# A chunked attention feeding a four-expert layer: the second pair's attention computed two tiles at a time

## The chip, the cores and the metric

The kernel runs on one core of one Trainium2 chip. The metric is the device time of one execution in microseconds (us). A tile is 128 tokens. TensorE is called PE in the profile (its weight loads PEld), VectorE DVE, ScalarE ACT, GpSimd POOL, and SyncE, whose queue issues all DMAs here, SP.

## The reference

Attention within chunks of 64 positions, then a mixture of four experts whose weights multiply every token:

```
scores = q_c @ k_c^T / 8            # 8 batches x 8 heads x 9 chunks, 64 x 64 each
attn   = exp(scores - rowmax); attn = attn / (rowsum + 1e-9)
x      = (attn @ v_c), heads side by side        # 4608 tokens x 512
p      = domain_probs / (rowsum + 1e-9)
out    = sum over e of p[:, e] * (relu(x @ w1[e]) @ w2[e])   # w1 512x1024, w2 1024x512
```

All inputs and outputs are float32.

## The kernel before

**Blocks and passes.** The 36 tiles are taken as one block of 512 tokens and then four pairs of blocks, 1024 tokens (8 tiles) to a pair. The code numbers the pairs 0 to 3; "the second pair" is pair 1. For every block or pair the kernel makes eight passes, n, one for each half of an expert's 1024 hidden columns: passes 0 to 7 belong to the first block, 8 to 15 to pair 0, 16 to 23 to pair 1, and so on to 39. While the passes of one pair run, the attention of the next pair is put between their products: pair 1's attention lies in passes 9 to 14, pair 2's in passes 17 to 21, pair 3's in 25 to 29.

**A pass.** Every float32 factor is split into a high and a low part (ACT rounds off `hi`, POOL or DVE subtracts to get `lo`), and a product is three matmuls for each 128 rows. In the pairs, blocks of 2 by 2 are multiplied with seven products instead of eight, which needs sums and differences of the blocks (`s1` to `s4` of the weights, `t1` to `t4` of the other side). A step is one such product: six matmuls of 128x512. A pass has 28 steps, in an order written out by hand; `g` and `h` are the two halves of x @ w1, `a` and `b` those of the second product for the pass before:

```
WOVEN = ("a1 g1 a2 g2 g6 a5 g5 a6 a3 g7 a7 g4 g3 a4 h1 h2 "
         "b1 b5 h6 b6 b3 h5 b7 h7 b2 b4 h4 h3").split()
```

Counted from 0, step 13 is `a4`, step 17 `b5`, step 20 `b3`, step 21 `h5`, step 22 `b7`, step 25 `b4`. `later_pass` keeps a table `at`: what hangs on step i is issued to the engines right after that step, in the order in which it was added to the table. Each engine works through its own queue in order. `a1, a6, a7, a4`, and likewise `b1, b6, b7, b4`, add up in one PSUM bank, A1; after each of them DVE adds the bank to an accumulator in SBUF (`Outer.add`, L983), and the next of the four may not write the bank before that read.

**w1's factors in pair 0.** In passes 9 to 14 the split factors of w1 are made on the chip. `half_load(n + 1, g)` loads a half of w1's raw blocks into `scratch`, a buffer of 4096 columns: 512 columns of its own (`scratch[0][:, :SUB]`) and then 14 pieces of 256 columns, seven for each half g. `half_sum` (L573, DVE) computes s1 to s4 into pieces; `make` (L590 on ACT, L591 on POOL) splits two pieces at a time, the seven units k = 0 to 6 at steps 20, 26 of a pass and 2, 8, 11, 14, 17 of the next, and `keep_made` stores them for the later pairs. Before, the loads of half 0 hang on step 5 and its sums on steps 11 or 15, 21, 21, 21; half 1's sums are DVE's at steps 9, 9, 10, 11 of the pass that uses them.

**Attention in pair 0's passes (pair 1's tiles).** One tile at a time (`attend`, `a_next`): a burst on PE holds the 16 64x64 products of one tile's `attn @ v` and the 16 of the next tile's scores, between two steps of the pass. It hangs on step 11 or 23, following TILES: nine bursts in all, the first with scores alone, the last with values alone. Between bursts: maximum and difference on DVE (L308, L313), exp on ACT (L319), sums and scaling and a 32x32 transpose on DVE (L322 to L329, L188), and `a_place`, five ACT copies from PSUM to SBUF (L194, L198). ACT copies the result to `scratch[0][:, :SUB]` (L221, L222), and SP stores it from there to `x_kept` in DRAM; pass 15 loads all of it back (`x_back`).

**Attention in the later passes (pairs 2 and 3).** `attend_two` takes two tiles to a burst, always behind step 12: values of tiles t-2 and t-1, scores of t and t+1; five bursts in all. Both tiles' scores lie in `psa`, two PSUM banks, the first tile in columns 0 to 255 of both, the second in 256 to 511. The first tile's softmax hangs on step 13, its scaling and transpose (`two_weights`) on 17, its `a_place` and then the second tile's softmax on 21, the second tile's weights and place on 6 and 9 of the next pass.

Of the kernel before, what the change touches and what calls it, by code (L numbers as in the profile page):

```python
# [15 lines left out]
P = 128  # L16
# [15 lines left out]
def chunk_attention_moe(ctx: ExitStack, tc: tile.TileContext, qk, v, v0, dp, w1, w2, out):  # L32
# [89 lines left out]

    def a_load_v(t, odd=(False, True)):
        s = st[t]
        if not odd[0]:
            s["v"] = load.tile([P, 2 * HG, C], F32, name="v_in")
        to, of = (
            a.rearrange("p (g i h) d -> p g i (h d)", g=2, i=2) for a in (s["v"], v[t - NT])
        )
        if not odd[0]:  # L130
            nc.sync.dma_start(out=to[:, :, 0], in_=of[:, :, 0])
        if odd[-1]:
            for half in range(2):
                rows, other = slice(half * C, (half + 1) * C), slice((1 - half) * C, (2 - half) * C)
                nc.sync.dma_start(out=to[rows, :, 1], in_=of[other, :, 1])

    def a_load_after(t):
        if (t + 1 - NT) % (PAIR * NT):
            a_load(t + 1)

    def quarters():
# [7 lines left out]
    def of_half(i):  # L149
        return slice(i * C, (i + 1) * C)  # L150
# [4 lines left out]

    def a_scores(t):
        s = st[t]
        s["sc"] = blocks(0)
        for c, half, slot, head in quarters():
            q, k = (s["x"][of_half(c), head // HG, x, head % HG] for x in range(2))  # L160
            nc.tensor.matmul(s["sc"][of_half(half), c, slot], lhsT=q, rhs=k, start=True, stop=True)  # L161

    def a_less_max(t):
# [8 lines left out]

    def a_sums(t):
        z = psa[:, 0, HG * C : HG * C + 2 * HG].rearrange("p (c j) -> p c j", c=2)
        st[t]["r"] = inverse_sums(st[t]["sc"], z)

    def a_scale(t):
# [3 lines left out]
        scale(s["e"], s["sc"], s["r"])  # L181

    def a_weights(t):
        a_sums(t)
        a_scale(t)

# [15 lines left out]

    def a_values(t):

        s = st.pop(t)
        av = blocks(1)
        for c, half, slot, head in quarters():
            nc.tensor.matmul(  # L208
                av[of_half(slot % 2), half, head // 2], lhsT=s["v"][of_half(half), head],
                rhs=s["pt"][of_half(half), c, slot], start=True, stop=True,  # L210
            )

    def a_copy(t):
        pair, i = divmod(t - NT, PAIR * NT)
        if pair == 1:
            tile_x = scratch[0][:, :SUB].rearrange("p (j q) -> p j q", j=NK)
        else:
            tile_x = of_tiles(pair, i, 1)[:, 0]
        to = tile_x.rearrange("p j (c q) -> p c j q", c=2)
        av = blocks(1)  # L220
        nc.scalar.copy(out=to[:, :, 0::2], in_=av[:, :, 0::2])  # L221
        nc.scalar.copy(out=to[:, :, 1::2], in_=av[:, ::-1, 1::2])  # L222
        if pair == 1:
            nc.sync.dma_start(out=x_kept[:, i], in_=tile_x)

# [8 lines left out]

    def two_load(t, i):
        if i == 0:
            a_load(t)
            return
        pair = (t - NT) // (PAIR * NT)
        to = of_tiles(pair, 6, 2).rearrange("p g (x i) (j s) -> p g x (i j) s", x=2, s=C)  # L240
        st[t] = {"x": to}
        nc.sync.dma_start(out=to, in_=qk[t].rearrange("g c d x h s -> (c d) g x h s"))

    def two_load_v(t, i, odd):
        if i and not odd:
            pair, j = divmod(t - NT, PAIR * NT)
            st[t]["v"] = of_tiles(pair, 7 if j == 7 else 5, 1)[:, 0].rearrange("p j (h d) -> p j h d", h=2)
        elif not odd:
            st[t]["v"] = load.tile([P, NK, 2, C], F32, name="v_in")
        to = st[t]["v"].rearrange("p (g i) h d -> p g i h d", i=2)  # L250
        of = v[t - NT].rearrange("p (g i h) d -> p g i h d", g=2, i=2)
        if not odd:
            nc.sync.dma_start(out=to[:, :, 0], in_=of[:, :, 0])
            return
        for half in range(2):
            rows, other = slice(half * C, (half + 1) * C), slice((1 - half) * C, (2 - half) * C)
            nc.sync.dma_start(out=to[rows, :, 1], in_=of[other, :, 1])
# [17 lines left out]
    def two_next(t, scores, banks=("B1", "C1")):  # L275
# [15 lines left out]
        if av:  # L291
            pair, j = divmod(t - NT, PAIR * NT)
            to = of_tiles(pair, j, 2).rearrange("p i j (c q) -> p i j c q", c=2)
            for half in range(2):
                for odd in range(2):
                    nc.scalar.copy(out=to[:, :, odd::2, half ^ odd], in_=av[half][:, :, odd::2])

    x_kept = dram.tile([P, PAIR * NT, NK, P], F32, name="x_kept")
# [32 lines left out]
    def attention(pair):  # L331
# [14 lines left out]
        for t in range(first, last, 2):  # L346
# [16 lines left out]
            two_next(t, t + 2 if t + 2 < last else None, (None, None))  # L363

    def a_next(t, after):

        if t is not None:
            a_values(t)
        if after is not None:
            a_scores(after)  # L370

        if t is not None:
            a_copy(t)

# [218 lines left out]
    def make_before(k):  # L598

        if not before:  # L600
            before.append(load.tile([P, 2, *UNIT[1:]], F32R, name="qk_in"))
        src, hi = staged.pop(0), before[0][:, k] if k < 2 else scratch[0][:, :SUB].bitcast(F32R).rearrange(
            "p (u b c) -> p u b c", u=2, c=P
        )
        nc.scalar.copy(out=hi, in_=src)
# [961 lines left out]
    def probs_load(n, s):  # L1567
# [17 lines left out]

    EARLY, LATE = (6, 9, 11), (17, 21, 24)
    TILES = {
        1: ((LATE, 0),), 2: ((EARLY, 1),), 3: ((EARLY, 2), (LATE, 3)), 4: ((EARLY, 4),),
        5: ((EARLY, 5), (LATE, 6)), 6: ((EARLY, 7),),
    }  # L1590
    ALONE = "a1 b1 a2 a5 b5 a6 b6 a3 b7 b2 a7 b3 a4 b4".split()
# [4 lines left out]

    def loads(at, i, t):

        for after, f in enumerate((
            lambda: a_load_v(t, (False,)), lambda: a_load_v(t, (True,)), lambda: a_load_after(t),  # L1600
        )):
            later.append((i + 2 + after, f)) if i + 2 + after >= len(WOVEN) else add(at, i + 2 + after, f)


    later = []

    def attend(at, pair, places, i):
        t = (1 + pair * PAIR) * NT + i
        after = t + 1 if i + 1 < PAIR * NT else None
        if i == 0:  # L1610
            add(at, 13, lambda: a_next(None, t))
            add(at, 14, lambda: a_softmax(t))
            loads(at, 13, t)
        add(at, places[0], lambda: a_weights(t), lambda: a_transpose(t))
        add(at, places[1], lambda: a_place(t))
        add(at, places[2], lambda: a_next(t, after))
        if after:
            add(at, places[2] + 1, lambda: a_softmax(after))
            loads(at, places[2], after)

    def attend_two(at, pair, r):

        t0 = (1 + pair * PAIR) * NT
        if r == 0:
            add(at, 12, lambda: two_load(t0 + 1, 1))
        if not 1 <= r <= 5:
            return
        t, burst = t0 + 2 * (r - 1), 12
        if r > 1:
# [3 lines left out]
        if r < 5:  # L1633
            add(at, burst + 1, lambda: a_softmax(t))
            add(at, 17, lambda: two_weights(t))
            add(at, 21, lambda: a_place(t), lambda: a_softmax(t + 1))
            for i in range(2):
                for odd in range(2):
                    add(at, burst + 2 + 2 * i + odd, lambda i=i, odd=odd: two_load_v(t + i, i, odd))
                if r < 4:  # L1640
                    add(at, burst + 6 + i, lambda i=i: two_load(t + 2 + i, i))
# [53 lines left out]
    def later_pass(n, ahead, late, held):  # L1695
# [247 lines left out]
```

## Time and profile before

| | |
|---|---|
| median of 3 runs | 1463.19 us (1462.77 to 1464.83) |
| profiled execution | 1462.92 us, its span 1461.1 us, 1.8 us around it |
| DVE, ACT, POOL busy over the span | 1080.0, 623.8, 975.8 us |
| pass 11 (302.5 to 343.4 us): PE, DVE, ACT, POOL busy | 40.88, 35.51, 21.36, 32.97 us |
| pass 18 (579.0 to 619.4 us): PE, DVE, ACT, POOL busy | 40.40, 31.16, 16.98, 22.04 us |
| DMA share of pass 11 and of pass 18 | 0.73 and 0.70 |

A row of the timeline has start and length in us, engine, line, operation, out<-in, count, and in brackets how long the engine stood idle before it and what ended that. A row of the chain has start, length and what ran. An `x6` of L758 is one step. f32 products are recorded as two instructions each, so 16 products are x32.

### The profile page before, as it was taken

The page shows a single profiled execution, that of the slowest core. Times are in us where ns is not written, and L with a number is a line of the kernel's source. Part 1 is how long each engine was busy: PE and PEld are TensorE (multiplying, and loading weights), DVE is VectorE, ACT ScalarE, POOL GpSimd, SP SyncE. Part 2 cuts the span into 40 slices and gives each one's busy share as a digit, 9 for nine tenths or more (in the row PEclk, how much of TensorE's full clock was granted, in tenths as well). Part 3 has the DMA queues.
Part 4 walks back from the last instruction along what each step waited for, and adds up shares of the span by engine and source line. Part 5 has one row for each costly group of instructions (what it writes and reads, how often), then busy time and mean ns, then how long its engine had stood idle before and what let it go on. Part 6 is the DMA issues. An engine that isn't in the chain of part 4 may idle for free.

```text
span 1461.1 us, 23404 instructions
## 1 busy us (share of the span) xinstructions
PE 1454.8 (100%) x8574; PEld 1198.8 (82%) x8574; DVE 1080.0 (74%) x1500; ACT 623.8 (43%) x1169; POOL 975.8 (67%) x728
## 2 busy tenths in 40 slices
PE   9999999999999999999999999999999999999998
PEld 7888888888888888888888888888888888888887
DVE  6566758888887986777767977777668856666666
ACT  5556545544554434444423434444334343223332
POOL 6878888888888775455557665655557655555555
PEclk9999999999999999999999999999999999999999
DMA  9899697868779689666565688675566785565555
GB/s 324 302 341 325 256 343 229 278 233 274 236 250 345 219 256 287 233 221 209 189 205 197 230 222 282 218 243 196 197 201 202 206 249 197 199 201 200 204 189 157
DMA packets 198994, 348.51 MB, mean 239 GB/s; under 512 B 70224, under 2 KB 109408, under 8 KB 198496
## 3 DMA queue, kind: packets, MB, share of 16 engines
q1 hardware_dynamic: 198880, 347.02, 72.1%
q8 instruction: 68, 1.11, 0.3%
q14 instruction: 46, 0.38, 0.1%
HBM read 275.59 MB, written 71.38 MB: 237 GB/s over the span
## 4 chain that ended last, share of the span: by engine, by line
PE 97%; POOL 1%; issue 1%; DVE 0%; DMA 0%; ACT 0%; SPq 0%; POOLq 0%; ACTq 0%
PE A L758 50%; PE C L758 27%; PE B L758 15%; POOL hf L448 1%; PE psa L264 1%; PE B L283 1%; PE psa L208 0%; DMA w<-hf 0%; POOL wf L448 0%; PE psa L161 0%; PE C L1256 0%; PE C L283 0%; PE C L1279 0%; PE A L1256 0%; PE B L1164 0%
## 5 line engine op out<-in xcount | busy, mean ns | idle before, releaser
L936 POOL TENSOR_TENSOR hf<-wraw,hf 128x512 fp32r<-128x512 f32 x384 | 508.1, 1341 | 226.3 <-ACT hf L933 225.1
L758 PE MATMUL A<-hf,wf 128*128 128x512 f32 x1536 | 391.4, 390 | 0.0
L758 PE MATMUL A<-xh,wf 128*128 128x512 f32 (+1 forms) x1120 | 386.9, 389 | 0.0
L933 ACT CAST hf<-wraw 128x512 fp32r<-128x512 f32 x384 | 233.3, 622 | 291.0 <-DVE wraw L927 99.5
L758 PEld LDWEIGHTS A<-hf,wf 128*128 128x128 f32 x1536 | 286.5, 188 | 61.9 <-DVE acc L983 1.9
L758 PEld LDWEIGHTS A<-xh,wf 128*128 128x128 f32 x1120 | 210.0, 188 | 43.9 <-POOL wf L591 0.3
L821 ACT COPY s<-A 128x512 f32<-128x512 f32 x192 | 112.7, 587 | 291.2 <-PE A L758 290.9
L758 PE MATMUL A<-xl,wf 128*128 128x512 f32 (+1 forms) x560 | 217.4, 388 | 0.0
L983 DVE TENSOR_TENSOR acc<-A,acc 128x512 f32<-128x512 f32 x232 | 157.9, 681 | 64.5 <-PE A L758 64.1
L758 PE MATMUL C<-xh,wf 128*128 128x512 f32 (+1 forms) x584 | 201.7, 389 | 0.1
L758 PE MATMUL C<-hf,wf 128*128 128x512 f32 x768 | 194.7, 389 | 0.0
L758 PEld LDWEIGHTS C<-hf,wf 128*128 128x128 f32 x768 | 144.2, 188 | 29.9
L758 PEld LDWEIGHTS C<-xh,wf 128*128 128x128 f32 x584 | 109.4, 188 | 23.2 <-DVE B L956 0.5
L927 POOL TENSOR_TENSOR wf<-wraw,wf 128x512 f32<-128x512 f32 x31 | 40.0, 1292 | 129.2 <-DVE wf L921 128.4
L758 PEld LDWEIGHTS A<-xl,wf 128*128 128x128 f32 x560 | 105.2, 188 | 21.7
L936 POOL TENSOR_TENSOR hf<-wf,hf 128x512 fp32r<-128x512 f32 x64 | 90.7, 1418 | 47.2 <-ACT hf L933 47.2
L758 PE MATMUL B<-xh,wf 128*128 128x512 f32 (+1 forms) x344 | 115.4, 384 | 0.0
L983 DVE TENSOR_TENSOR acc<-C,acc 128x512 f32<-128x512 f32 x120 | 82.7, 689 | 43.2 <-PE C L758 40.3
L758 PE MATMUL C<-xl,wf 128*128 128x512 f32 (+1 forms) x292 | 113.3, 388 | 0.0
L927 DVE TENSOR_TENSOR wraw<-wf,wraw 128x512 f32<-128x512 f32 x64 | 94.7, 1479 | 5.5 <-POOL hf L936 4.3
L758 PE MATMUL B<-hf,wf 128*128 128x512 f32 x384 | 97.8, 390 | 0.0
L927 POOL TENSOR_TENSOR wraw<-wraw 128x512 f32<-128x512 f32 x63 | 91.8, 1458 | 0.0
(255 smaller groups left out, 1982.1 us busy)
## 6 DMA issues: line engine op xcount, KB each, us to landing
wf<-w SPq DMA_DIRECT2D x402, 512.0 KB, 4.2
w<-wf SPq DMA_DIRECT2D x46, 512.0 KB, 5.3
w<-hf SPq DMA_DIRECT2D x28, 512.0 KB, 6.6
w<-hf SPq DMA_DIRECT2D x42, 256.0 KB, 5.3
qk_in<-in_qk SPq DMA_DIRECT2D x20, 512.0 KB, 6.1
wf<-in_w SPq DMA_DIRECT2D x19, 512.0 KB, 6.5
xraw<-in_qk SPq DMA_DIRECT2D x14, 512.0 KB, 7.3
ws<-p_t SPq DMA_DIRECT2D x24, 256.0 KB, 4.1
```

Of the source, the lines that this page charges most:

```text
L264: nc.tensor.matmul(s["sc"][of_half(half), c, slot], lhsT=q, rhs=k, start=True, stop=True)
L283: nc.tensor.matmul(av[half][of_half(slot % 2), i, head // 2], lhsT=s["v"][of_half(half), head // 2, head % 2], rhs=s["pt"][of_half(half), ...
L448: eng.tensor_tensor(out=t[1], in0=src, in1=t[0].bitcast(F32), op=ALU.subtract)
L758: nc.tensor.matmul(out, lhsT=lhs(k, a), rhs=rhs(k, b), start=first and i == 0, stop=last and i == len(parts) - 1, skip_group_check=not (fi ...
L821: nc.scalar.copy(out=t, in_=self.a)
L927: (eng or nc.vector).tensor_tensor(out=self.values[place, k], in0=self.values[a, k], in1=self.values[b, k], op=op)
L933: nc.scalar.copy(out=self.part(name, 0)[:, k], in_=self.values[name, k])
L936: (eng or nc.gpsimd).tensor_tensor(out=self.part(name, 1)[:, k], in0=self.values[name, k], in1=self.part(name, 0)[:, k].bitcast(F32), op=A ...
L983: nc.vector.tensor_tensor(out=acc[key], in0=src, in1=acc[key], op=ALU.add)
```

## The change

Pair 1 takes `attend_two` as well, with five bursts, in passes 10 to 14, behind step 13 instead of 12. The second tile of a burst has no buffer of its own: its q and k go to pieces 0 to 3, loaded in halves at steps 22 and 27 of the pass before (behind the makes at 20 and 26 that read these pieces), its v to pieces 4 and 5 at steps 3 and 4 (behind the make at step 2). The result of the first tile goes to the 512 columns in front, that of the second to pieces 2 and 3 (the last burst: 4 and 5), and one DMA stores both.

Since pieces 0 to 5 are taken until the burst, the loads of half 0 of w1 move from step 5 to step 13, behind the burst, and s1 of half 0 from 11 or 15 to 20. Half 1's sums go from DVE to POOL in passes 10 to 14. In pass 14 three raw loads of w2 go to pieces at steps 3, 4 and 10 instead of `e`, `pt`, `v_in` at 9, 12, 12, and the third made unit goes to `v_in`. Pass 9 keeps its old places for w1. The single-tile functions (`attend`, `a_next`, `a_values`, `a_copy` and others) are gone.

```
+        if pair == 1:
+            if groups.start == 0:
+                to = pieces(0, 4).rearrange("p a b c -> p (a b c)")
+                st[t] = {"x": to.rearrange("p (g x h s) -> p g x h s", g=2, x=2, h=HG)}
+            nc.sync.dma_start(
+                out=st[t]["x"][:, groups],
+                in_=qk[t, groups].rearrange("g c d x h s -> (c d) g x h s"),
+            )
+            return
...
+            if pair == 1:
+                to = pieces(4, 2).rearrange("p a b c -> p (a b) c")
...
+                n = 3 * SUB if j == PAIR * NT - 2 else 2 * SUB
+                two = scratch[0][:, : 2 * n].rearrange("p (i x) -> p i x", i=2)[:, :, :SUB]
...
+            if pair == 1:
+                nc.sync.dma_start(out=x_kept[:, j : j + 2], in_=two)
...
     def attend_two(at, pair, r):
         t0 = (1 + pair * PAIR) * NT
-        if r == 0:
+        if pair == 1:
+            if 0 <= r <= 3:
+                for g, i in enumerate((22, 27)):
+                    add(at, i, lambda g=g: two_load(t0 + 2 * r + 1, 1, slice(g, g + 1)))
+            if 1 < r <= 5:
+                for odd in range(2):
+                    add(at, 3 + odd, lambda odd=odd: two_load_v(t0 + 2 * r - 3, 1, odd))
+        elif r == 0:
             add(at, 12, lambda: two_load(t0 + 1, 1))
         if not 1 <= r <= 5:
             return
-        t, burst = t0 + 2 * (r - 1), 12
+        t, burst = t0 + 2 * (r - 1), 13 if pair == 1 else 12
...
-            for i in range(2):
+            for i in range(1 if pair == 1 else 2):
...
         elif pair == 0:
-            for places, i in TILES.get(n % n_pass, ()):
-                attend(at, pair + 1, (17, 20, 23) if places == LATE else places, i)
+            attend_two(at, pair + 1, n % n_pass - 1)
...
         if n + 1 < 2 * n_pass - 1:
-            add(at, 5, lambda: half_load(n + 1, 0))
+            add(at, 5 if n == n_pass + 1 else 13, lambda: half_load(n + 1, 0))
             add(at, 13, lambda: half_load(n + 1, 1, (0,)))
             add(at, 19, lambda: half_load(n + 1, 1, (1,)))
-            half_sums(at, 0, (11 if n % n_pass in (3, 5) else 15, 21, 21, 21))
+            half_sums(at, 0, (15 if n == n_pass + 1 else 20, 21, 21, 21))
         if n_pass < n < 2 * n_pass - 1:
-            half_sums(first, 1, (5, 6, 9, 10) if n == n_pass + 1 else (9, 9, 10, 11))
             if n == n_pass + 1:
+                half_sums(first, 1, (5, 6, 9, 10))
                 half_sums(first, 0, (None, None, None, 3))
+            else:
+                half_sums(first, 1, (9, 9, 10, 11), nc.gpsimd)
...
-            (2 * n_pass - 2, (), ((9, att, "e"), (12, att, "pt"), (12, load, "v_in"))),
+            (2 * n_pass - 2, (), ((3, None, 0), (4, None, 2), (10, None, 6))),
```

More of the change, by code (lines that the diff above doesn't have):

```diff
@@ L121, in a_load @@
         nc.sync.dma_start(out=s["x"], in_=qk[t].rearrange("g c d x h s -> (c d) g x h s"))
[L123 to L139, printed above, removed]
     def quarters():
@@ L154, in blocks @@
         return psa[:, :, i * HG * C : (i + 1) * HG * C].rearrange("p c (j k) -> p c j k", k=C)
[L156 to L161, printed above, removed]
     def a_less_max(t):
@@ L171, in a_softmax @@
         a_exps(t)
-    def a_sums(t):
-        z = psa[:, 0, HG * C : HG * C + 2 * HG].rearrange("p (c j) -> p c j", c=2)
-        st[t]["r"] = inverse_sums(st[t]["sc"], z)
     def a_scale(t):
@@ L181, in a_scale @@
         scale(s["e"], s["sc"], s["r"])
-    def a_weights(t):
-        a_sums(t)
-        a_scale(t)
     def a_transpose(t):
@@ L201, in a_place @@
                 )
[L203 to L224, printed above, removed]
     def x_tiles(pair):
@@ L233, in of_tiles, with two_load @@
         return (xraw[pair] if pair in xraw else x_tiles(pair))[:, i : i + n]
-    def two_load(t, i):
+    def two_load(t, i, groups=slice(0, 2)):
         if i == 0:
@@ L246, in two_load_v @@
             pair, j = divmod(t - NT, PAIR * NT)
-            st[t]["v"] = of_tiles(pair, 7 if j == 7 else 5, 1)[:, 0].rearrange("p j (h d) -> p j h d", h=2)
+            if pair == 1:
+                to = pieces(4, 2).rearrange("p a b c -> p (a b) c")
+            else:
+                to = of_tiles(pair, 7 if j == 7 else 5, 1)[:, 0]
+            st[t]["v"] = to.rearrange("p j (h d) -> p j h d", h=2)
         elif not odd:
@@ L292, in two_next @@
             pair, j = divmod(t - NT, PAIR * NT)
-            to = of_tiles(pair, j, 2).rearrange("p i j (c q) -> p i j c q", c=2)
+            if pair == 1:
+                n = 3 * SUB if j == PAIR * NT - 2 else 2 * SUB
+                two = scratch[0][:, : 2 * n].rearrange("p (i x) -> p i x", i=2)[:, :, :SUB]
+                two = two.rearrange("p i (j q) -> p i j q", j=NK)
+            else:
+                two = of_tiles(pair, j, 2)
+            to = two.rearrange("p i j (c q) -> p i j c q", c=2)
             for half in range(2):
@@ L363, in attention @@
             two_next(t, t + 2 if t + 2 < last else None, (None, None))
[L365 to L373, printed above, removed]
     KEYS = {"a11": 0, "a12": 1, "a22": 2, "s1": 3, "s2": 4, "s3": 5, "s4": 6}
@@ L598, in make_before @@
     def make_before(k):
[L600 to L604, printed above, removed]
+        if k == 0:
+            t = load.tile([P, 2, *UNIT[1:]], F32R, name="qk_in")
+            before.extend(t[:, i] for i in range(2))
+        elif k == 2:
+            before.append(load.tile(UNIT, F32R, name="v_in"))
+        src, hi = staged.pop(0), before[k]
         nc.scalar.copy(out=hi, in_=src)
@@ L625, in raw_load @@
     def raw_load(pool, name):
-        k, t = unstaged.pop(0), pool.tile([P, 2, 2, P], F32, name=name)
+        k, t = unstaged.pop(0), pool.tile([P, 2, 2, P], F32, name=name) if pool else pieces(name, 2)
         staged.append(t)
@@ L1583, in chunk_attention_moe @@
     )
[L1586 to L1590, printed above, removed]
     ALONE = "a1 b1 a2 a5 b5 a6 b6 a3 b7 b2 a7 b3 a4 b4".split()
@@ L1595, in first_load @@
             a_load((1 + pair * PAIR) * NT)
[L1597 to L1602, printed above, removed]
-    later = []
[L1607 to L1619, printed above, removed]
+    later = []
     def attend_two(at, pair, r):
         t0 = (1 + pair * PAIR) * NT
-        if r == 0:
+        if pair == 1:
+            if 0 <= r <= 3:
[5 more added lines that the diff above has]
+        elif r == 0:
             add(at, 12, lambda: two_load(t0 + 1, 1))
@@ L1737, in later_pass @@
         elif pair == 0:
-            for places, i in TILES.get(n % n_pass, ()):
-                attend(at, pair + 1, (17, 20, 23) if places == LATE else places, i)
+            attend_two(at, pair + 1, n % n_pass - 1)
         late = []
         if n + 1 < 2 * n_pass - 1:
-            add(at, 5, lambda: half_load(n + 1, 0))
+            add(at, 5 if n == n_pass + 1 else 13, lambda: half_load(n + 1, 0))
             add(at, 13, lambda: half_load(n + 1, 1, (0,)))
             add(at, 19, lambda: half_load(n + 1, 1, (1,)))
-            half_sums(at, 0, (11 if n % n_pass in (3, 5) else 15, 21, 21, 21))
+            half_sums(at, 0, (15 if n == n_pass + 1 else 20, 21, 21, 21))
         if n_pass < n < 2 * n_pass - 1:
-            half_sums(first, 1, (5, 6, 9, 10) if n == n_pass + 1 else (9, 9, 10, 11))
             if n == n_pass + 1:
+                half_sums(first, 1, (5, 6, 9, 10))
                 half_sums(first, 0, (None, None, None, 3))
+            else:
+                half_sums(first, 1, (9, 9, 10, 11), nc.gpsimd)
             for i in (3, 8, *MAKE_AT[2:]) if n == n_pass + 1 else MAKE_AT:
```

## The prediction

> **What bounds the kernel now.** I read the page first, then the chain of work that ended last, then TensorE's bursts in it, and last the queues of the other engines around the second group of steps of a pass.
>
> ```profile
> span 1461.1 us, 23404 instructions
> PE 1454.8 (100%) x8574; PEld 1198.8 (82%) x8574; DVE 1080.0 (74%) x1500; ACT 623.8 (43%) x1169; POOL 975.8 (67%) x728
> PE 97%; POOL 1%; issue 1%; DVE 0%; DMA 0%; ACT 0%; SPq 0%; POOLq 0%; ACTq 0%
> ```
>
> PE is never idle for long and the chain is PE for 97% of the span. So two things alone can move the time: what PE itself takes for the attention, and a new place where PE waits. The averages of the other engines say nothing about the second; that is read from the pass.
>
> **The bursts, from the chain.** A step is 1.36 us (x12 below is two steps). A burst costs the time of its own rows, plus what the step behind it takes over 1.36.
>
> ```profile
> 241.66 0.67 PE psa L161 x30
> 242.33 1.58 PE A L758 x6
> ...
> 253.45 2.72 PE A L758 x12
> 256.17 0.62 PE psa L208 x32
> ...
> 257.32 1.59 PE B L758 x6
> ...
> 279.32 0.66 PE psa L208 x32
> ...
> 280.51 1.58 PE C L758 x6
> ...
> 318.81 0.02 issue
> ...
> 320.05 1.58 PE C L758 x6
> ...
> 440.17 0.66 PE psa L208 x32
> 440.83 1.60 PE C L758 x6
> ```
>
> Scores alone: 0.67 + 0.22 = 0.89. Behind step 23: 257.32 - 256.17 = 1.15, + 0.23 = 1.38. Behind step 11: 1.19 + 0.22 = 1.41 in pass 10, 1.24 + 0.22 = 1.46 in pass 11, where PE also waits for the weights that ACT places just ahead. Values alone: 0.66 + 0.24 = 0.90. Step 23 holds three bursts (passes 9, 11, 13), step 11 four (10 and 12 like the one, 11 and 13 like the other), and the first and last make nine: 0.89 + 3 x 1.38 + 2 x 1.41 + 2 x 1.46 + 0.90 = 11.7 us.
>
> What the new form costs is shown by the third pair's attention, which has it already:
>
> ```profile
> 557.18 1.14 PE psa L264 x62
> 558.32 2.73 PE A L758 x11
> ...
> 596.64 0.20 PE B L283
> ...
> 598.72 2.28 PE A L758 x9
> ...
> 717.89 0.20 PE B L283
> ...
> 718.98 2.04 PE A L758 x8
> ```
>
> At 0.227 for one matmul (1.36 / 6), eleven take 2.49, nine 2.04, eight 1.81. So scores alone: 1.14 + 0.24 = 1.38; full: 2.08 + 0.24 = 2.32; values alone: 1.09 + 0.23 = 1.32. Five bursts: 1.38 + 3 x 2.32 + 1.32 = 9.7 us. **Term one: 11.7 - 9.7 = 2.0 us saved.** The products are the same; what goes is four times the way into and out of the small products. That is 0.14% of the kernel; about 0.2%, 2.9 us, is what a measurement here can tell from no change. So the gain alone stays inside it, and the waits decide.
>
> **What gets late: DVE in steps 17 to 25.** This is the part I take to decide. In the new form DVE's queue reads: `b5`'s add, the first tile's weights (step 17), t2, `b6`'s and `b3`'s adds, s1 (step 20), then from step 21 the second tile's softmax, then s2, s3, s4, and only then `b7`'s add. The sums stand behind the softmax because they are put into the table after it. The third pair's attention has all of this but the sums. Its pass 18, by the timeline:
>
> ```profile
> 612.88 0.69 DVE L308 TENSOR_REDUCE m<-psa 128x8 f32<-128x512 f32 x1 [1.88 <-ACT pt L198]
> 613.61 0.70 DVE L313 TENSOR_TENSOR psa<-psa,m 128x512 f32<-128x512 f32 x1
> 614.22 0.68 DVE L983 TENSOR_TENSOR acc<-A,acc 128x512 f32<-128x512 f32 x1
> ```
> ```profile
> 615.13 1.52 PE L758 MATMUL A<-hf,wf 128*128 128x512 f32 x6
> ```
> ```profile
> 611.36 1.49 ACT L198 COPY pt<-psa 32x256 f32<-32x256 f32 x4
> ```
> ```profile
> DVE m L308 <- ACT pt L198: 15.1, 8, 1.9
> ```
>
> The second tile's softmax does not start until ACT has placed the first tile (611.36 + 1.49 = 612.85), though it reads other columns of psa; it is so 8 times of 8, four in each of the two pairs, 1.88 us each. Then come its two operations, then `b7`'s add, 614.22 to 614.90. `b4`, which writes the same bank next, is due at 615.13. So there are 0.23 us to spare, and the change puts three sums in between. The Trainium skill's page "PSUM — Partial Sum Buffer", section "Terms", says that two engines on one bank and quadrant at once are an error. By that this wait stays in any arrangement with both tiles in the same two banks; the eight rows agree.
>
> That PE does wait for such an add is seen in pass 15:
>
> ```profile
> 475.73 0.68 DVE L983 TENSOR_TENSOR acc<-A,acc 128x512 f32<-128x512 f32 x1
> ```
> ```profile
> 476.46 1.23 PEld L758 LDWEIGHTS A<-hf,wf 128*128 128x128 f32 x6 [0.43 <-DVE acc L983]
> ```
>
> The add ends at 476.41 and the next product in the bank starts 0.05 later. Now the prices of what goes in between, all from pass 11 of before:
>
> ```profile
> 318.22 0.88 DVE L573 TENSOR_TENSOR xraw<-xraw 128x256 f32<-128x256 f32 x2
> ...
> 333.58 2.83 DVE L573 TENSOR_TENSOR xraw<-xraw 128x256 f32<-128x256 f32 x3
> 336.34 0.68 DVE L983 TENSOR_TENSOR acc<-A,acc 128x512 f32<-128x512 f32 x1
> ```
> ```profile
> 333.06 2.73 POOL L936 TENSOR_TENSOR hf<-wraw,hf 128x512 fp32r<-128x512 f32 x2 [1.46 <-ACT hf L933]
> ```
> ```profile
> 335.54 0.62 ACT L590 CAST wf<-xraw 128x512 fp32r<-128x512 f32 x1
> ```
>
> Two sums took 0.88 with POOL idle, so three are 1.3; three beside POOL's subtractions took 2.83. ACT has one operation more ahead of the place than in pass 18, the rounding of step 20's unit, 0.62. In pass 18's times: the place ends at 612.85 + 0.6 = 613.5; softmax 1.34 (612.88 to 614.22), to 614.8; three sums alone, to 616.1; `b7`'s add 0.68, to 616.8. `b4` is due at 615.13: it waits 1.7 us. With the sums at 2.83 the add ends at 618.35 and the wait is 3.2. In pass 11 of before the same sums hurt nobody: no softmax stood ahead of them, and `b7`'s add (336.34 to 337.02) made it to `b4`, which was held back by the burst behind step 23 besides.
>
> Which price? In pass 18 POOL was without work there:
>
> ```profile
> 615.71 1.29 POOL L936 TENSOR_TENSOR hf<-wf,hf 128x512 fp32r<-128x512 f32 x1 [2.76 <-ACT hf L933]
> ```
>
> It waits 2.76 for ACT, whose rounding comes after the same softmax's exp. In pair 0 one unit's subtraction more (about 1.3, as the next rows show) goes into this gap and leaves 1.5, about what three lone sums take. So I take 1.7. The page "SBUF — State Buffer", section "Who interferes with whom", says that a DVE operation with two SBUF inputs and a POOL operation reading SBUF block each other whole; the 0.88 for two against 2.83 for three agree, and if it bit here in full the second price would hold (the rival below). s1 costs nothing: it falls into the 1.88 that DVE stands waiting for the place.
>
> This happens in passes 10 to 13, which have both a second softmax and sums of the next pass. **Term two: 4 x 1.7 = 6.8 us lost**, bounds 0 (DVE is otherwise early enough) and 4 x 3.2 = 12.8.
>
> **What I take at nothing, and its cover.** Half 1's four sums on POOL:
>
> ```profile
> 309.49 1.30 POOL L591 TENSOR_TENSOR wf<-xraw,wf 128x512 fp32r<-128x512 f32 x1
> ...
> 316.99 1.31 POOL L591 TENSOR_TENSOR wf<-xraw,wf 128x512 fp32r<-128x512 f32 x1
> 321.34 1.28 POOL L591 TENSOR_TENSOR wf<-xraw,wf 128x512 fp32r<-128x512 f32 x1 [3.04 <-ACT wf L590]
> ```
>
> No row shows such a sum on POOL. Half the elements of a 1.3 us operation give 0.65 each, 2.6 for four; as long as whole ones they would be 5.2. They follow 316.99's unit, and POOL then stands idle 3.04, because ACT rounds the next unit only after the burst's copies. That burst goes to step 13, so the unit itself comes no later than now. With 5.2 it would be 2 us late, still ahead of `h2`: unit done at 318.3 + 5.2 + 1.3 = 324.8, `h2` due with two more steps and a full burst at 320.05 + 3 x 1.36 + 0.9 = 325.0. No cost, up to 0.5 at the worst. DVE's relief lies where it has room, so it gains nothing.
>
> SP: the load of v at steps 3 and 4 waits for the unit that POOL finishes at 309.49 + 1.30 = 310.8; the loads behind it in SP's queue wait too, the next pair of w2 units among them. The pass began at 318.81 - 12 x 1.36 = 302.5, so the burst is due at 302.5 + 14 x 1.36 = 321.5.
>
> ```profile
> xraw<-in_w SPq DMA_DIRECT2D x19, 256.0 KB, 4.3
> v_in<-in_v SPq DMA_DIRECT2D x8, 128.0 KB, 3.5
> ```
> ```profile
> 324.28 1.26 SPq L135 DMA_DIRECT2D v_in<-in_v  x2
> ```
>
> Three issues in a row at 0.63 each, and 3.5 to landing: v is there by about 316, 5 us early. Half 0's raw loads, now behind the burst and behind the store of x on SP, land about 4.3 after some 3 us, 7 behind the burst; s1 comes 10 to 11 behind it (in pass 18, DVE is through `b3` at 611, and 598.72 + 1.36 is step 14's start). Held by 3 us. Pass 14's and 15's edits move loads where no wait of PE stands now.
>
> **Sum.** -2.0 + 6.8 = +4.8 on the profiled execution's 1462.92 (span 1461.1 and 1.8 around): 1467.7. The median of the runs is 0.3 above it: 1468.0.
>
> **Rivals.**
> 1. *The sums are covered and only the bursts count.* Place: `b7`'s add in passes 10 to 13; price 0; it decides if ACT's place ends before about 611.8 in pass 18's times (1.34 + 1.3 + 0.68 = 3.3 ahead of 615.13), or if the softmax need not wait for it. Against it: eight waits of 1.88. For it: DVE is idle just before, so nothing but this one wait is late. Time 1463.19 - 2.0 = 1461.2, not slower.
> 2. *The sums meet POOL.* If POOL runs a little later than I take it, they cost 2.83 again and the wait is 3.2: -2.0 + 12.8 = +10.8, 1474.0.
> 3. *The bursts do not do what is said*, since v or the second half of q and k is late: they hang on POOL's units and on SP. Each of four bursts then waits. 5 us of room speak against it; at 1 us each, on top of the forecast, 1472.
> 4. *More goes than I count*: PE's waits in pass 9 and 15 (some 0.3 us each) and pressure on DVE early in the pass. With no new wait, 1460.
>
> **How the numbers follow.** Forecast 0.47, rival 1 0.28, rival 2 0.15, rival 3 0.05, rival 4 0.05. The forecast itself runs from a wait of 1.1 (rounding hidden) to 2.2 (one sum beside POOL), +2.4 to +6.8, and one eighth of it falls below +2.9. Slower: 0.41 + 0.15 + 0.05 = 0.61. Faster by over 2.9: part of rival 4 and a little of 1, 0.07. Same: 0.32. Range 1461.0 to 1474.0, from the one rival to the other; most of the likeliest case alone lies in 1465.6 to 1470.
>
> **What would show it.** Right: the groups of waits have PEld waiting for DVE acc L983 four more times at 1 to 3 us, in passes 10 to 13, three steps before the pass ends; DVE m L308 waiting for ACT pt 12 times instead of 8; the bursts L264 and L283 in five places between 280 and 450, costing 9.7. Wrong: passes 11 to 13 each 40.4 us long (28 x 1.36 + 2.32) with no wait but the burst, or a wait of PE at another row, first of all for POOL wf L591 at the start of a pass.

## The result and the profile after

| | before | after |
|---|---|---|
| median | 1463.35 us (1462.77 to 1464.83) | 1471.61 us (1469.88 to 1472.44) |
| ratio to before | | 1.0054, 95% interval 1.0041 to 1.0067 |
| profiled execution, its span | 1462.92, 1461.1 | 1472.01, 1470.2 |

The change costs 8.3 us; 4.8 were forecast. Lines have moved: L758 is L711 after, L983 L936, L308 L275, L198 L165, L573 L525, L591 L543, L264 L222, L283 L241, L927 L880, L933 L886, L936 L889, L821 L774.

From the page: PE's busy time grew by 0.9 us, the span by 9.1, and PE's share of the chain, 97% before, is 88%.

```profile
PE 1455.7 (99%) x8574; PEld 1197.1 (81%) x8574; DVE 1069.0 (73%) x1480; ACT 624.5 (42%) x1169; POOL 986.2 (67%) x748
PE 88%; POOL 4%; DVE 3%; DMA 2%; ACT 1%; issue 1%; SPq 0%; POOLq 0%; ACTq 0%; DVEq 0%
```

Where PE waits is shown by the waits of its loads between 222 and 510 us, where passes 9 to 15 lie (columns: us in all, times, longest). Before:

```profile
PEld A L758 <- DVE acc L983: 0.7, 2, 0.4
...
PEld A L758 <- POOL wf L591: 0.3, 1, 0.3
```

After:

```profile
PEld A L711 <- DVE acc L936: 9.1, 10, 1.7
PEld A L711 <- POOL wf L543: 4.2, 6, 0.9
```

The first group holds the forecast waits at `b4`. Pass 11, from DVE's and PE's timelines of after:

```profile
334.97 1.06 DVE L525 TENSOR_TENSOR xraw<-xraw 128x256 f32<-128x256 f32 x1
337.45 0.69 DVE L275 TENSOR_REDUCE m<-psa 128x8 f32<-128x512 f32 x1 [1.42 <-ACT pt L165]
338.17 0.70 DVE L280 TENSOR_TENSOR psa<-psa,m 128x512 f32<-128x512 f32 x1
338.78 1.08 DVE L525 TENSOR_TENSOR xraw<-xraw 128x256 f32<-128x256 f32 x3
339.78 0.68 DVE L936 TENSOR_TENSOR acc<-A,acc 128x512 f32<-128x512 f32 x1
340.38 1.71 DVE L880 TENSOR_TENSOR wraw<-wraw 128x512 f32<-128x512 f32 x1
```
```profile
337.81 1.52 PE L711 MATMUL B<-hf,wf 128*128 128x512 f32 x6
340.52 1.66 PE L711 MATMUL A<-hf,wf 128*128 128x512 f32 x6 [1.19 <-DVE acc L936]
...
350.47 0.39 PE L711 MATMUL A<-xl,wf 128*128 128x512 f32 x1
351.33 0.73 PE L711 MATMUL A<-xh,wf 128*128 128x512 f32 x2 [0.47 <-POOL wf L543]
```

It is the queue of the forecast, row for row: s1 in the gap, the second softmax behind the place, three sums, `b7`'s add. `b4` was due at 337.81 + 1.36 = 339.17 and starts at 340.52: 1.35 late, and its next matmul another 0.11 (0.34 behind it in place of 0.227). So in each of passes 10 to 13: 1.46, 5.8 us in all.

The last two rows are the second group, a wait that the sum did not have: `g6`, step 4 of the next pass, goes on at 351.33 where 350.47 + 0.23 = 350.70 was due. With the 0.11 behind it 0.74, four times (0.70 to 0.75), 2.9 us. It waits for a unit of w1 from POOL, whose timeline reads:

```profile
340.26 1.28 POOL L889 TENSOR_TENSOR hf<-wf,hf 128x512 fp32r<-128x512 f32 x1 [1.84 <-ACT hf L886]
342.82 5.06 POOL L889 TENSOR_TENSOR hf<-wraw,hf 128x512 fp32r<-128x512 f32 x4 [1.28 <-ACT hf L886]
...
349.54 1.74 POOL L543 TENSOR_TENSOR wf<-xraw,wf 128x512 fp32r<-128x512 f32 x1
```

POOL stands idle twice for ACT's roundings and then runs without a gap to that unit. The second gap follows from DVE: the sum of 340.38 stands behind `b7`'s add and takes 1.71 beside POOL's subtraction; ACT rounds its result, POOL subtracts. So one delay on DVE is paid in two places, at `b4` and 11 us later at `g6`.

The bursts, from the chain of after (scores alone, then a full one; what lies between two rows is the burst and one step):

```profile
280.27 1.14 PE psa L222 x62
...
282.99 1.38 PE B L711 x6
...
322.05 0.20 PE B L241
...
325.71 1.38 PE B L711 x6
```

282.99 - 280.27 - 1.36 = 1.36, and 325.71 - 322.05 - 1.36 = 2.30. Over all matmul starts, counting what is above 0.227 from one to the next, the nine bursts of before cost 11.4 and the five of after 9.5.

One more wait differs, in pass 15, where DVE copies x out of the scratch once it has come back from DRAM. Before, then after:

```profile
473.64 2.17 DVE L704 TENSOR_TENSOR qk_in<-xraw 128x1024 f32<-128x1024 f32 x1 [1.90 <-DMA wf<-w]
```
```profile
483.01 1.83 DVE L657 TENSOR_TENSOR qk_in<-xraw 128x1024 f32<-128x1024 f32 x1 [3.48 <-DMA wf<-w]
```

The add behind it holds PE 0.28 before and 1.53 after. By the same count of starts, the 9.1 us between 222 and 510 are: bursts -1.9, `b4` +5.8, `g6` +2.9, pass 15 +1.25, and 1.0 in waits under 0.35 each. Outside that stretch the two kernels differ by 0.1.

### The profile page after: what moved, and what is told of

Same layout as the page of the kernel before. It is cut to its first block, busy times and chain, and to the rows that moved or that the text cites. A ratio compares the mean times of both kernels' runs of the same rounds, so it can differ in the third digit from the quotient of the medians.

```text
span 1470.2 us, 23417 instructions
## 1 busy us (share of the span) xinstructions
PE 1455.7 (99%) x8574; PEld 1197.1 (81%) x8574; DVE 1069.0 (73%) x1480; ACT 624.5 (42%) x1169; POOL 986.2 (67%) x748
## 4 chain that ended last, share of the span: by engine, by line
PE 88%; POOL 4%; DVE 3%; DMA 2%; ACT 1%; issue 1%; SPq 0%; POOLq 0%; ACTq 0%; DVEq 0%
PE A L711 45%; PE C L711 25%; PE B L711 14%; POOL hf L889 1%; PE psa L222 1%; POOL hf L400 1%; POOL wf L543 1%; PE B L241 1%; DMA w<-xraw 1%; DMA xraw<-x_kept 1%; DVE wraw L880 1%; ACT pt L165 0%; DMA wf<-w 0%; DVE acc L936 0%; ACT hf L886 0%
## 5 line engine op out<-in xcount | busy, mean ns | idle before, releaser
L889 POOL TENSOR_TENSOR hf<-wraw,hf 128x512 fp32r<-128x512 f32 x384 | 507.5, 1341 | 232.3 <-ACT hf L886 231.0
L711 PE MATMUL A<-hf,wf 128*128 128x512 f32 x1536 | 392.2, 391 | 6.0 <-DVE acc L936 6.0
L711 PE MATMUL A<-xh,wf 128*128 128x512 f32 (+1 forms) x1120 | 388.1, 390 | 1.8 <-POOL wf L543 1.8
L886 ACT CAST hf<-wraw 128x512 fp32r<-128x512 f32 x384 | 233.4, 622 | 301.8 <-DVE wraw L880 108.0
L711 PEld LDWEIGHTS A<-hf,wf 128*128 128x128 f32 x1536 | 285.9, 188 | 69.8 <-DVE acc L936 10.3
L711 PEld LDWEIGHTS A<-xh,wf 128*128 128x128 f32 x1120 | 209.6, 188 | 47.8 <-POOL wf L543 4.2
L774 ACT COPY s<-A 128x512 f32<-128x512 f32 x192 | 112.6, 587 | 287.8 <-PE A L711 287.1
L711 PE MATMUL A<-xl,wf 128*128 128x512 f32 (+1 forms) x560 | 217.5, 388 | 0.0
L936 DVE TENSOR_TENSOR acc<-A,acc 128x512 f32<-128x512 f32 x232 | 157.7, 680 | 66.0 <-PE A L711 65.7
L711 PE MATMUL C<-xh,wf 128*128 128x512 f32 (+1 forms) x584 | 201.1, 388 | 0.1
L711 PE MATMUL C<-hf,wf 128*128 128x512 f32 x768 | 194.8, 389 | 0.0
L711 PEld LDWEIGHTS C<-hf,wf 128*128 128x128 f32 x768 | 144.2, 188 | 30.0
L711 PEld LDWEIGHTS C<-xh,wf 128*128 128x128 f32 x584 | 109.5, 188 | 22.9 <-DVE B L909 0.5
L889 POOL TENSOR_TENSOR hf<-wf,hf 128x512 fp32r<-128x512 f32 x64 | 89.2, 1393 | 54.6 <-ACT hf L886 54.6
L880 POOL TENSOR_TENSOR wf<-wraw,wf 128x512 f32<-128x512 f32 x31 | 40.0, 1289 | 127.7 <-DVE wf L874 126.9
L711 PEld LDWEIGHTS A<-xl,wf 128*128 128x128 f32 x560 | 105.2, 188 | 21.7
L711 PE MATMUL B<-xh,wf 128*128 128x512 f32 (+1 forms) x344 | 115.5, 384 | 0.0
L936 DVE TENSOR_TENSOR acc<-C,acc 128x512 f32<-128x512 f32 x120 | 82.6, 689 | 42.9 <-PE C L711 40.1
L711 PE MATMUL C<-xl,wf 128*128 128x512 f32 (+1 forms) x292 | 113.2, 388 | 0.0
L880 DVE TENSOR_TENSOR wraw<-wf,wraw 128x512 f32<-128x512 f32 x64 | 95.1, 1486 | 7.1 <-POOL hf L889 6.0
L711 PE MATMUL B<-hf,wf 128*128 128x512 f32 x384 | 97.7, 389 | 0.0
L880 POOL TENSOR_TENSOR wraw<-wraw 128x512 f32<-128x512 f32 x63 | 93.1, 1478 | 0.0
```

Of the source, the lines that this page charges most:

```text
L711: nc.tensor.matmul(out, lhsT=lhs(k, a), rhs=rhs(k, b), start=first and i == 0, stop=last and i == len(parts) - 1, skip_group_check=not (fi ...
L774: nc.scalar.copy(out=t, in_=self.a)
L880: (eng or nc.vector).tensor_tensor(out=self.values[place, k], in0=self.values[a, k], in1=self.values[b, k], op=op)
L886: nc.scalar.copy(out=self.part(name, 0)[:, k], in_=self.values[name, k])
L889: (eng or nc.gpsimd).tensor_tensor(out=self.part(name, 1)[:, k], in0=self.values[name, k], in1=self.part(name, 0)[:, k].bitcast(F32), op=A ...
L936: nc.vector.tensor_tensor(out=acc[key], in0=src, in1=acc[key], op=ALU.add)
```

## The experiments

All are edits of after. Theory A is the prediction's: what stands ahead of `b7`'s add on DVE makes the waits. Rival B seeks the cause of `g6`'s waits on POOL (half 1's sums put there, or POOL's own queue), rival C seeks the whole cause in the wait for the place; theory D is told where it comes in. Rival D in the expectations of softmax_both and both_w16 is another one, DVE's load over the whole pass. What the expectations call `a2` in the later runs is the step that PE does behind `b4`, `h4`.

| kernel | median us (range) | ratio to before, 95% |
|---|---|---|
| sums_late | 1488.45 (1486.67 to 1488.91) | 1.0168 [1.0153, 1.0183] |
| sums_pool | 1470.97 (1470.49 to 1471.83) | 1.0052 [1.0037, 1.0067] |
| half1_dve | 1471.42 (1471.24 to 1471.59) | 1.0054 [1.0039, 1.0069] |
| softmax_first | 1468.64 (1467.61 to 1469.43) | 1.0033 [1.0021, 1.0046] |
| softmax_both | 1478.01 (1476.79 to 1478.97) | 1.0098 [1.0083, 1.0113] |
| both_w16 | 1478.5 (1475.85 to 1479.57) | 1.0098 [1.0081, 1.0115] |
| softmax_late | 1480.7 (1478.77 to 1483.93) | 1.0119 [1.0104, 1.0134] |
| sums_behind | 1471.23 (1466.96 to 1472.73) | 1.0049 [1.0036, 1.0061] |
| behind_first | 1474.28 (1471.68 to 1474.76) | 1.0069 [1.0057, 1.0081] |
| split | 1466.93 (1466.58 to 1468.05) | 1.0025 [1.0015, 1.0034] |
| split_first | 1468.01 (1467.82 to 1469.23) | 1.0035 [1.0022, 1.0047] |
| best | 1466.55 (1465.8 to 1468.14) | 1.0022 [1.0012, 1.0031] |

**The sums behind the add: sums_late.**

```
-half_sums(at, 0, (... 20, 21, 21, 21))
+half_sums(at, 0, (15, 21, 21, 21) if n == n_pass + 1 else (20, 23, 25, 27))
```

> Half 0's s2, s3, s4 of passes 10 to 13 go from step 21 (ahead of b7's add in DVE's queue) to steps 23, 25 and 27, behind it. Theory A (the queue order on DVE: the second softmax waits for ACT's place, and the three sums, 1.08 us together, stand between it and b7's add): b7's add comes 1.0 us earlier, PE's four waits at b4 fall from 1.46 to about 0.4 each; the four waits at g6 for POOL's unit stay near 0.7, since the sums still stand among the adds that feed POOL. In all about 4 us less than the changed kernel's 1471.6: 1467.5. Rival C (the softmax's wait for the place is the whole cause, the sums ride along): the waits at b4 stay at 1.4 or more, the time at 1471.

By step 23 the pieces already hold q and k of the next pair of tiles, so these sums read q and k in place of w1's blocks, and they wait for that load (DVE's waits, 222 to 510):

```profile
DVE xraw L525 <- DMA xraw<-in_qk: 23.2, 6, 5.2
```

The time says nothing on A, for the edit made a wait of its own. The `b4` waits fell to 0.45, as A said.

**The sums on POOL, and half 1's sums back on DVE: sums_pool, half1_dve.**

```
+half_sums(at, 0, (15 if n == n_pass + 1 else 20, None, None, None))          # sums_pool
+half_sums(at, 0, (None, 21, 21, 21), None if n == n_pass + 1 else nc.gpsimd)
...
-half_sums(first, 1, (9, 9, 10, 11), nc.gpsimd)                               # half1_dve
+half_sums(first, 1, (9, 9, 10, 11))
```

> Half 0's s2, s3, s4 of passes 10 to 13 run on POOL, still at step 21. Theory A: the waits at b4 fall from 1.46 to about 0.4, as with the sums late; on POOL three sums at 0.73 (2.2 us) fall into gaps of 1.84 and 1.28 that it has there, so the waits at g6 do not grow: about 1467. Rival B (the waits at g6 come from POOL having too much work since it took over half 1's sums): 2.2 us more work makes these waits grow by 1 to 2 us each, and the time stays at 1471 or grows.

> Undoes one part alone: half 1's four sums of passes 10 to 14 are DVE's again. Theory A: both engines have room at these steps (POOL stands 3.04 us idle behind them), so the waits at b4 (1.46) and at g6 (0.73) stay and the time stays within 1 us of 1471.6. Rival B (POOL's added sums cause the waits at g6): these four waits, 2.9 us in all, go, 1468.7.

PE in sums_pool, pass 11 (`b4`, `a2`, `g6`):

```profile
339.26 1.66 PE L711 MATMUL A<-hf,wf 128*128 128x512 f32 x6 [0.18 <-DVE acc L936]
...
347.48 0.73 PE L711 MATMUL B<-hf,wf 128*128 128x512 f32 x2 [0.20 <-POOL hf L889]
...
350.88 0.74 PE L711 MATMUL A<-xh,wf 128*128 128x512 f32 x2 [0.81 <-POOL wf L543]
```

With the three sums gone from DVE, `b4`'s wait went from 1.46 to 0.45: they are the cause of 1.0 of it. But the time stayed, as rival B said, and A's 1467 missed: POOL takes 2.57 for the three, and the waits for it grew from 0.74 to 1.10 at `g6` and from nothing to 0.46 at `a2`. PE in half1_dve, the same `b4`:

```profile
341.06 1.19 PE L711 MATMUL A<-hf,wf 128*128 128x512 f32 x4 [1.19 <-DVE acc L936]
```

It waits as in after, and `g6` too (0.73), though POOL has four operations less. Half 1's sums on POOL cost nothing; that part of rival B falls, while POOL's own queue stays a cause where more is put on it. Pass 15's wait was 0.28 in both runs.

**The second softmax ahead of the place: softmax_first.**

```
-add(at, 21, lambda: a_place(t), lambda: a_softmax(t + 1))
+two = [lambda: a_place(t), lambda: a_softmax(t + 1)]
+add(at, 21, *(two[::-1] if pair == 1 else two))
```

> In pair 1's attention the second tile's softmax is put ahead of the first tile's place at step 21, so that DVE need not wait for ACT there (1.42 us a pass). Theory A, with the sums' price taken from DVE and POOL together: the softmax ends about 1.4 earlier, but the three sums then run beside POOL's subtractions and cost up to 2.8 in place of 1.08, so b7's add gains little or nothing and the waits at b4 stay between 1.0 and 1.9; 1470 to 1472. Rival C (the wait for the place is the cause): b7's add comes 1.4 earlier and the waits at b4 are gone, 5.9 us less: 1465.7.

DVE's timeline (the softmax stands at 335.86 with no idle time before it):

```profile
337.18 2.10 DVE L525 TENSOR_TENSOR xraw<-xraw 128x256 f32<-128x256 f32 x3
339.21 0.68 DVE L936 TENSOR_TENSOR acc<-A,acc 128x512 f32<-128x512 f32 x1
```

The wait for the place is gone, 1.42 of it, but the add is only 0.5 earlier against `b4`, whose wait is 0.97: the same three sums took 2.10 in place of 1.08, because they now run while POOL is at work. The waiting had kept them out of its way. The time, 1468.64, lies between A's 1470 and C's 1465.7; pass 15's wait, 0.28 here, is 1.25 of the gain. A price of the sums that POOL's work sets is the prediction's second price, and it is theory D.

**The softmax moved far: softmax_both, both_w16, softmax_late.**

```
+add(at, burst + 1, lambda: a_softmax(t + 1))            # softmax_both: pair 1, with the first tile's
-add(at, 17, lambda: two_weights(t))                     # both_w16: besides
+add(at, 16 if pair == 1 else 17, lambda: two_weights(t))
+add(at, 23 if pair == 1 else 21, lambda: a_softmax(t + 1))   # softmax_late, alone
```

> In pair 1's attention the second tile's softmax goes from step 21 to step 14, right behind the first tile's, where DVE stands idle for 1.49 us; the sums stay where the change put them. It waits there for no place of ACT, and 1.34 of work and 1.42 of idle time leave the stretch ahead of b7's add. Theory A: the sums now run beside POOL and cost 2.8 in place of 1.08, so of 2.76 about 1.0 is won: b4 waits 0.4 instead of 1.46, g6 0.1 to 0.3 instead of 0.73; 1464 to 1466. Rival C (the wait for the place was the whole cause): b4 waits not at all, and g6 neither: 1461.4, faster than before. Rival D (the time comes from DVE's load over the whole pass, not from its order): no change, 1471.6.

> As the kernel with both softmaxes at step 14, and the first tile's weights at step 16 instead of 17, so that DVE's remaining idle time ahead of b5's add (0.56) is used and the sums start 0.5 earlier. Theory A: b4's wait goes from 0.4 to 0 or 0.1, g6 to 0.1; the time is then before's less the bursts' 2.0 and plus some 0.5 to 1 left at g6: 1462 to 1463.5, within 0.2 % of before. Rival D: no change, 1471.6.

> The second tile's softmax goes from step 21 to step 23, behind b7's add, nothing else. Theory A: the sums follow s1 at once, beside POOL, and cost 2.8 in place of 1.08; with the softmax's 1.34 and the 1.42 of idle time out of the way b7's add comes 1.0 earlier, so b4 waits 0.4. The softmax now delays the adds and subtractions that feed POOL at the end of the pass, so g6 keeps 0.5 to 0.8: 1466 to 1468. If only the number of DVE's operations ahead of b7's add mattered (each at its lone price, 1.08 for the sums), b4 would not wait at all, 1465.

All three missed by far, and rival D's "no change" with them. DVE and POOL in softmax_both:

```profile
337.24 5.65 DVE L525 TENSOR_TENSOR xraw<-xraw 128x256 f32<-128x256 f32 x4
```
```profile
337.04 2.72 POOL L889 TENSOR_TENSOR hf<-wraw,hf 128x512 fp32r<-128x512 f32 x2
339.73 1.48 POOL L543 TENSOR_TENSOR wf<-xraw,wf 128x512 fp32r<-128x512 f32 x1
341.16 1.44 POOL L889 TENSOR_TENSOR hf<-wf,hf 128x512 fp32r<-128x512 f32 x1
```

Four sums beside four operations of POOL: 1.41 each, where three alone took 1.08 together. `b4` waits 2.5. In softmax_late the four took 5.35 and `b4` waits 1.9; in both_w16 PE waited at `b3` as well (1.2 to 1.5). Theory A had the place of the wait; the price of a sum depends on what POOL does meanwhile. The Trainium skill's page "SBUF — State Buffer", section "Who interferes with whom", has a DVE operation with two SBUF inputs and a reading POOL operation shut each other out for a whole instruction. One sum for each POOL operation in these rows agrees.

**The sums behind the add, cleanly: sums_behind, behind_first.**

```
-for g, i in enumerate((22, 27)):
+for g, i in enumerate((27, 27)):
-half_sums(at, 0, (... 20, 21, 21, 21))
+half_sums(at, 0, (15, 21, 21, 21) if n == n_pass + 1 else (20, 23, 25, 26))
+(behind_first: the edit of softmax_first too)
```

> Half 0's last three sums at steps 23, 25 and 26, behind b7's add, and both parts of the second tile's q and k loaded at step 27, so that nothing is overwritten. Theory A (the three sums in front of b7's add make the wait at b4): the add comes 1.08 earlier, PE waits 0.4 at b4, 4 x 1.0 are gained, 1467 to 1468. Theory D (the sums cost what POOL lets them: DVE is without a gap from 340 to 353, and three sums beside POOL's subtractions cost 1.4 each): b4 falls to 0.4 all the same, but the units behind them are late by some 3, PE waits over 1 at g6 or a2 of the next group, and the time is 1470 or more.

> As the run before, and the second tile's softmax ahead of the first tile's place. Theory A: no wait at b4 (0 to 0.1), 1464 to 1466. Theory D: no wait at b4 either, but waits at g6 and a2 as in the run before, 1468 or more.

Measured: `b4` waits 0.46 and 0, as both theories said, and the time is no better than after. PE in sums_behind, then in behind_first:

```profile
344.98 1.66 PE L711 MATMUL A<-hf,wf 128*128 128x512 f32 x6 [0.47 <-DVE acc L936]
```
```profile
342.60 0.50 PE L711 MATMUL A<-xh,wf 128*128 128x512 f32 x1 [0.74 <-ACT s L774]
...
346.09 1.66 PE L711 MATMUL A<-hf,wf 128*128 128x512 f32 x6 [0.48 <-DVE acc L936]
```

The waits moved to `a1`, now held by `b4`'s own add, and to `h4`, held by ACT, which places before it copies; `g6` waits 0.85 in two passes of four in the one kernel, in one in the other, and nothing in the rest. DVE has no gap from 340 to 353 in which the sums are free. D named `g6` and `a2` as the places of the new waits; `g6` waits in no more than two passes of four, and `a1` was not named. So the time that D gave (1470 or more) came in part by other waits, in sums_behind with pass 15's 1.53 among them.

**Shared between the two engines: split, split_first.**

```
+half_sums(at, 0, (15 if n == n_pass + 1 else 20, 21, None, None))
+half_sums(at, 0, (None, None, 21, 21), None if n == n_pass + 1 else nc.gpsimd)
+(split_first: the edit of softmax_first too)
```

> Half 0's second sum stays on DVE behind the softmax, the third and fourth go to POOL, which stands idle 1.84 there. Theory A: b7's add comes 0.72 earlier, b4 waits 0.7. Theory D: two sums on POOL (about 1.6) fit into the 1.84, so POOL's run of subtractions starts when it did and g6 waits 0.5 or less, unlike with all three on POOL (1.1): 1467 to 1468.5. If POOL is late even so, g6 stays at 0.7 or grows, and the time is 1469 to 1470.

> As the run before, and the second tile's softmax ahead of the first tile's place. Then the softmax runs by 335.9 to 337.2, one sum, and b7's add ends by 339.3: no wait at b4 by either theory. Theory D adds: with no more than one sum beside POOL's subtractions, g6 waits 0.4 or less and a2 nothing; 1464 to 1466. If the two sums on POOL delay its run, g6 and a2 wait 0.7 and more together and the time is 1467 or more.

DVE, POOL and PE in split:

```profile
337.63 0.62 DVE L525 TENSOR_TENSOR xraw<-xraw 128x256 f32<-128x256 f32 x1
338.16 0.68 DVE L936 TENSOR_TENSOR acc<-A,acc 128x512 f32<-128x512 f32 x1
338.76 0.83 DVE L880 TENSOR_TENSOR wraw<-wraw 128x512 f32<-128x512 f32 x1
```
```profile
337.23 0.73 POOL L525 TENSOR_TENSOR xraw<-xraw 128x256 f32<-128x256 f32 x1
338.32 0.73 POOL L525 TENSOR_TENSOR xraw<-xraw 128x256 f32<-128x256 f32 x1 [0.36 <-DVE xraw L525]
339.12 1.64 POOL L889 TENSOR_TENSOR hf<-wf,hf 128x512 fp32r<-128x512 f32 x1
340.72 5.04 POOL L889 TENSOR_TENSOR hf<-wraw,hf 128x512 fp32r<-128x512 f32 x4
```
```profile
338.90 1.66 PE L711 MATMUL A<-hf,wf 128*128 128x512 f32 x6 [0.73 <-DVE acc L936]
```

1466.93 us, 4.7 below after. Both waits fell: `b4` to 1.0, `g6` to 0.31, 3.6 us in four passes; another 1.25 is pass 15's wait, 0.28 here, which nothing ties to this edit. Two sums fit into the gap in which POOL had waited for ACT, and its run of four begins 1.82 behind `b4` (340.72 - 338.90) where it was 2.30 in after (342.82 - 340.52): 0.48 less, and `g6` waits 0.43 less. The run now follows POOL's own work without a gap, where in after it stood waiting for ACT and DVE. That ties `g6` in after to DVE's lateness. In split_first `b4` fell to 0.30, but ACT's copy for `h4` came 0.68 late and `g6` stood at 0.52: the time is 1.1 above split.

**All of it: best.**

```
+add(at, 21, lambda: a_less_max(t + 1), lambda: a_place(t), lambda: a_exps(t + 1))
+half 0's sums: s1 and s3 on POOL at 18, s2 on DVE at 21, s4 on POOL at 21
```

> All that the runs before point to: half 0's first and third sums on POOL at step 18, in its gap of 1.47 before the pair of subtractions; the second tile's maximum and difference on DVE ahead of the first tile's place, and its exp on ACT behind the place; then the second sum on DVE and the fourth on POOL. Theory A and D together: b7's add comes as soon as its products are done, ACT's copy for a2 no later than with the place first, POOL's run no later than in the run with two sums on POOL: waits at b4, a2 and g6 0 to 0.3 in all per pass, and the burst's 2.0 stay: 1461.5 to 1463.5. If the sums on POOL at step 18 push its pair of subtractions back (they take over 0.73 each beside DVE), a3 or b3 waits and the time is 1464 or more.

PE's timeline, then a row of POOL's and one of ACT's:

```profile
337.81 1.52 PE L711 MATMUL A<-hf,wf 128*128 128x512 f32 x6
339.49 0.50 PE L711 MATMUL A<-xh,wf 128*128 128x512 f32 x1 [0.16 <-ACT s L774]
...
348.79 0.50 PE L711 MATMUL A<-xh,wf 128*128 128x512 f32 x1 [0.34 <-POOL wf L543]
```
```profile
340.28 5.06 POOL L889 TENSOR_TENSOR hf<-wraw,hf 128x512 fp32r<-128x512 f32 x4
```
```profile
335.58 0.59 ACT L161 COPY pt<-psa 128x512 f32<-128x512 f32 x1 [1.01 <-DVE psa L280]
```

No wait at `b4` in any pass: with place and sums both out of the way of the add, it is gone, which shows the forecast's cause of that wait whole. But `h4` waits 0.43 for ACT and `g6` 0.63 for POOL, and one burst took 0.7 longer. 1466.55, where 1463.5 at most was expected: no better than split, 3.3 above before (ratio 1.0022 [1.0012, 1.0031]). No version found beats before.

Why less than `b4`'s wait is won shows beside after and split. POOL's run of four begins 3.65 behind the time at which `b4` was due in after (342.82 - 339.17), 2.71 in split (340.72 - 338.01) and 2.47 in best (340.28 - 337.81). The waits at `b4`, `h4` and `g6` together are 2.20, 1.31 and 1.06, each time 1.4 less; softmax_first and split_first fit too (2.93 in both, 1.47 and 1.50). So in these kernels the start of that run sets what PE loses in a pass; what it does not wait at `b4` it waits at `h4` or `g6`.

## Why the prediction was right

The sign and the mechanism held: slower, by a wait of `b4` for `b7`'s add in passes 10 to 13. The size was too small: 1471.6 lies inside the range only because that reached up to rival 2; it is above the 1465.6 to 1470 of the likeliest case and nearer to rival 2's 1474.0, whose cause was not there. By its steps:

- **Bursts, -2.0.** Measured -1.9, and 1.36 and 2.30 for the forms put at 1.38 and 2.32.
- **`b4`, 4 x 1.7.** 4 x 1.46. The softmax began 339.17 - 337.45 = 1.72 ahead of `b4`'s due time, 2.25 in pass 18: 0.53 lost to the rounding, 0.6 was taken. The three sums took 1.08 for 1.3. That POOL would be without work just then was read rightly: 338.42 to 340.26 is such a gap. So rival 2's price did not come, but the experiments met it as soon as the sums were moved into POOL's work. Rival 1 falls; the softmax did wait for the place (1.42 each, 12 such waits in the trace for 8 before). That this wait stays in any arrangement went too far: in best, with both tiles in the same banks, DVE goes first without waiting, and ACT's place waits 1.01 for it instead.
- **What follows the add.** The term that was missed: 2.9 at `g6`. The sum ended at `b4`, as if PE's wait there gave the others back their time. It doesn't, if the late engine has a queue behind the late operation: DVE's next sum, ACT's rounding and POOL's run shifted more than PE, and POOL's run sets the total. The prediction named this wait only as a sign of its being wrong.
- **Half 1's sums on POOL, nothing.** Right: half1_dve undid it and changed neither wait. Four took 2.93 on POOL, 2.6 was taken.
- **SP, v, q and k, nothing.** Right in after: all three full bursts cost 2.28, and rival 3 falls. In five of the edits one full burst took 0.4 to 0.7 longer (0.7 in best), but not for a late load: in best v has landed by 356.2, the burst begins at 362.18, and PE waits 0.43 ahead of its last recorded product for nothing that the profile shows.
- **Pass 14's and 15's edits, nothing.** Pass 15 cost 1.25 in the profile of after. All twelve experiments keep these edits; in nine of them the wait was 0.28 as before, in sums_late, softmax_late and sums_behind about 1.5. The edits alone don't make it. In after the copy begins 0.74 later against PE's work than in half1_dve and takes 1.83 for 1.31; why stays open.

-2.0 + 6.8 was to be -1.9 + 5.8 + 2.9 and some 2 more of pass 15 and small waits; that is why the profile shows 9.1 and not 4.8. Not tried: the two tiles' scores in different banks.

## What to carry to other kernels

A saving on the engine that bounds is worth only what the engines behind it leave: here 2 us of bursts, paid for with 8.7 us of waits at two steps, that no engine's busy share foretold. When an operation on a side engine is found late, follow it past the first wait that it causes, through the operations queued behind it and the engines that read them, to the next step that needs them. And move cheap operations between engines by their gaps: the same sum cost 0.36 in one engine's gap and 1.4 beside the other's work.

## What the runs showed of the hardware

Behind long waits PE ran at half its rate for a while. softmax_both, PE behind the wait at `b4`, and TensorE by stretches (columns: stretch, its length, PE busy, granted clock, DMA share, GB/s):

```profile
343.54 2.16 PE L711 MATMUL A<-hf,wf 128*128 128x512 f32 x6 [2.27 <-DVE acc L936]
345.49 0.63 PE L711 MATMUL A<-xh,wf 128*128 128x512 f32 x1
345.92 0.63 PE L711 MATMUL A<-xl,wf 128*128 128x512 f32 x1
```
```profile
325.00:341.00 16.00, 16.00 (x137) 1.00 0.81 262
...
343.50:346.00 2.50, 2.46 (x8) 0.70 0.87 348
346.00:350.00 4.00, 4.00 (x15) 0.76 0.83 249
```

Matmuls start 0.43 apart (345.92 - 345.49) in place of 0.227, seven or eight of them here, about 1.6 us in all. The granted clock of the stretch is 0.70, and 0.51 from 345 to 348 us. Over all runs, with 2.66 us from the last start to the next this came in three of four passes, with 2.25 to 2.27 in two of three, with 3.3 and more always; with 2.03 and less never. So a gap of 2.25 us and more from start to start can cost PE more than its length, and part of the time of softmax_both, both_w16 and sums_late is that. The Trainium skill's page "TensorE: Matmul & The Clock Gate", Part 1, has the clock halved behind an idle window of about 3.4 us. The halved rate agrees; here it came after less.
